# A fused attention and MLP kernel: q and k of the first eight blocks loaded in groups of four tokens, and another order of the opening

## The chip, the cores and the metric

The kernel runs on one core of a Trainium2 chip. The metric is the device time of one execution in microseconds; the median of 3 runs before the change is 1161.43 us (1158.59 to 1162.66). The engines are named as in the profile: PE (TensorE, with PEld for its weight loads), DVE (VectorE), ACT (ScalarE), POOL (GpSimd) and SP (SyncE, which here only issues DMAs).

## The reference, cut to what matters

Attention in chunks over q, k, v of shape 4 x 8 heads x 768 tokens x 64, then two MLPs of 512 x 2048 x 512 on the 3072 tokens. The weights are given in double precision.

```python
chunk, left_ctx, right_ctx = 32, 16, 8          # n_mem = 8
for c in range(nc):
    l_start = max(0, c_start - left_ctx)
    r_end = min(S, c_end + right_ctx)
    k_full = np.concatenate([mem_k, k[:, :, l_start:r_end]], axis=2)
    v_full = np.concatenate([mem_v, v[:, :, l_start:r_end]], axis=2)
    scores = scale * np.matmul(q_c, k_full.transpose(0, 1, 3, 2))
    scores = scores - np.max(scores, axis=-1, keepdims=True)
    a = np.exp(scores)
    a = a / (np.sum(a, axis=-1, keepdims=True) + 1e-09)
    out[:, :, c_start:c_end] = np.matmul(a, v_full)
...
h = x @ w_in;  x = np.maximum(0.01 * h, h) @ w_out           # first MLP
h = x @ w_in2; g = P(h) / (Q(h) + 1e-06); return g @ w_out2  # second MLP
```

Each chunk of 32 queries sees 64 keys: 8 memory rows and a span of 56 tokens (16 to its left, its own 32, 8 to its right). Spans of neighbouring chunks overlap by 24 tokens.

## The kernel before, in words

**MLP.** Tokens are cut into six tiles of 512. For every tile and each of 16 slices f of the hidden width, `emit_h` (L633) makes a bank hps of 128 x 512 by 12 matmuls (4 parts of the input width times three products of high and low halves: xh, xl for the activations, wih, wil for the weights), `leaky` (L645) turns it into gh and gl, and `emit_y` (L689) adds 12 matmuls into four banks acc. That is an item c; layer 0 has 96 of them, layer 1 another 96 (`rational` L656, `emit_o` L726). The items run in one loop (L792). Every item has two slots, 2c and 2c + 1: `wide(slot)` (L619) inserts attention work into slot 2c, which stands behind an `emit_h` and ahead of an `emit_y`, and into slot 2c + 1, behind that `emit_y`.

**Weights.** A half (w_in or w_out of one slice) is loaded by `load_w` (ld, L120) into one of three buffers wr, then `scale_w` (sc, ACT L139), `join_w` (jn, two DVE passes L153 and L156), `split_w` (ca, ACT L167, the high part) and the low part (lo, DVE L170). In the first token tile `weights0` (L180) does one such round twice per item, and a load waits until the join has freed its buffer. The high and low parts stand in 16 homes of their own for each of four kinds (`wpool`, L81).

**Attention.** A block j has 128 tokens of all 8 heads, four chunks; blocks 0 to 3 are the first token tile and are made in the opening, blocks 4 to 7 during the first token tile's items, the others later by another path (`wide_*`) which the change leaves alone. The steps of a block are: loads of q, k, v (q.ld, k.ld, v.ld); a, where PE transposes q and k (L319, L326) and ACT copies them to qT and kwT (L332, L335); s, the 64 small matmuls of scores (L347) and DVE's maximum and, for blocks 0 to 3, subtraction (L361, L363); e, the exponentials on ACT (L370, or eight short ones with their sums, L375, for blocks 4 to 7); n, DVE's normalisation (L384 to L389); p, four transposes of the weights by PE into a bank pst (L396) and ACT's copy pm (L400); x, 64 small matmuls with v (L414), ACT's copy to xh (L427) and DVE's xl (L431). q is loaded token by token, 256 bytes a piece, as 128 rows; k twice as 88 rows (a half block with its context), with memory rows above and below; v as eight loads of 56 rows, and memory rows by POOL's DMAs. Three places (`room`, L239) hold k and v of the blocks in turn; kwT and pwT are one buffer each.

**Order.** All engines run in the order in which the program issues. In the opening that is the list `OPENING` (L21): each word is one step of one block or of the weights. SP issues the loads in the list's order too. From block 4 on, `plan` (L578) puts block j's a into slot u = 1 + 6(j - 4), s and the next block's loads of q and k into u + 1, e into u + 2, n into u + 3, and p and x into the next block's u and u + 1, for block 7 into u + 4 and u + 5. Of PSUM's eight banks, four (acc) serve the MLP's sums and, in the opening, scores and x; the other four (ps) serve hps, the transposes, and blocks 4 to 7.

Of the kernel before, what the change touches and what calls it, by code (L numbers as in the profile page):

```python
# [30 lines left out]
def kernel(  # L31
# [49 lines left out]
    wpool = ctx.enter_context(tc.tile_pool(name="wpool", bufs=FC))  # L81
# [16 lines left out]
    small = const.tile([P, 14], F32, name="small")  # L98
    coef, ncf, babs = small[:, 0:6], small[:, 6:10], small[:, 10:12]
# [138 lines left out]
    spare = [xpool.tile([P, 2, 2 * H * D], F32R, tag=t, name=t).bitcast(F32) for t in ("xh", "xl")]  # L238
    room = [(kw, vflat), (spare[0][:, 0], spare[0][:, 1]), (spare[1][:, 0], spare[1][:, 1])]  # L239
    mem_in = {}  # L240
    mq, mqT, mm = {}, {}, {}

    def home(j):
        return j if j < len(room) else 0

    def mem_rows(kind, j, bi):
        if mem_in.get((kind, home(j))) == bi:
            return False
        mem_in[kind, home(j)] = bi
        return True  # L250

    def mid_load_q(j):
        bi, blk = divmod(j, WPS)
        if j < FIRST:
            t = wpool.tile([P, H * D], F32, tag=("wih", "wil", "woh", "wol")[j], name="q0")
        else:
            t = raw.tile([P, H * D], F32, tag="qr", name="qr", bufs=1)
        nc.sync.dma_start(out=t.rearrange("p (h d) -> p h d", h=H),
                          in_=q[bi, :, blk * P:(blk + 1) * P, :].rearrange("h p d -> p h d"))
        mq[j] = t  # L260

    def mid_mem_k(j):
        bi = j // WPS
        t = room[home(j)][0].rearrange("p (n h d) -> p n h d", n=2, h=H)
        if mem_rows("k", j, bi):
            for n in range(2):
                for row in (0, NM + CTX):
                    nc.gpsimd.dma_start(out=t[row:row + NM, n], in_=mem_k[bi].rearrange("h p d -> p h d"))

    def mid_load_k(j):  # L270
        bi, blk = divmod(j, WPS)
        mid_mem_k(j)
        t = room[home(j)][0].rearrange("p (n h d) -> p n h d", n=2, h=H)
        for n in range(2):
            at = blk * P + n * 2 * CHUNK - LCTX
            lo, hi = max(at, 0), min(at + CTX, S)
            nc.sync.dma_start(out=t[NM + lo - at:NM + hi - at, n],  # L277
                              in_=k[bi, :, lo:hi, :].rearrange("h p d -> p h d"))

    def mid_mem_v(j):  # L280
        bi = j // WPS
        t = room[home(j)][1].rearrange("p (n k h d) -> p k n h d", n=2, k=2, h=H // 2)
        W = WIN - NM
        if mem_rows("v", j, bi):
            for hh in range(2):
                for odd in range(2):
                    row = hh * WIN + odd * W
                    for n in range(2):
                        nc.gpsimd.dma_start(out=t[row:row + NM, odd, n],
                                            in_=mem_v[bi, 4 * hh:4 * hh + 4].rearrange("h p d -> p h d"))  # L290

    def mid_load_v(j):
        bi, blk = divmod(j, WPS)
        mid_mem_v(j)
        t = room[home(j)][1].rearrange("p (n k h d) -> p k n h d", n=2, k=2, h=H // 2)
        W = WIN - NM
        for hh in range(2):
            hs = slice(4 * hh, 4 * hh + 4)
            for odd in range(2):
                row = hh * WIN + (0 if odd else NM)  # L300
                at = blk * P + odd * CHUNK - LCTX
                for n in range(2):
                    a0 = at + n * 2 * CHUNK
                    lo, hi = max(a0, 0), min(a0 + W, S)
                    nc.sync.dma_start(out=t[row + lo - a0:row + hi - a0, odd, n],
                                      in_=v[bi, hs, lo:hi, :].rearrange("h p d -> p h d"))
# [7 lines left out]

    def mid_a_pe(j):
        t = mq.pop(j)
        ps = psw.tile([P, 512], F32, tag="ps", name="psq")
        for p in range(NP):
            nc.tensor.transpose(ps[:, p * P:(p + 1) * P], t[:, p * P:(p + 1) * P], ident)  # L319
        held["a", j] = [ps]  # L320
        t = room[home(j)][0]
        for n in range(2):
            ps = psw.tile([P, 512], F32, tag="ps", name="psk")[:, :NP * KW]
            for p in range(NP):
                f = n * H * D + p * P
                nc.tensor.transpose(ps[:, p * KW:(p + 1) * KW], t[:KW, f:f + P], ident[:KW, :KW])  # L326
            held["a", j].append(ps)

    def mid_a_act(j):
        psq, *psk = held.pop(("a", j))  # L330
        o = tmp.tile([P, NP, P], F32, tag="A", name="qT")
        nc.scalar.mul(out=o.rearrange("p c m -> p (c m)"), in_=psq, mul=scale)  # L332
        mqT[j] = o
        for n in range(2):
            nc.scalar.copy(out=kwT[:, n * NP * KW:(n + 1) * NP * KW], in_=psk[n])  # L335

    def mid_s_pe(j):
        qt = mqT.pop(j)
        kt = kwT[:, :2 * NP * KW].rearrange("p (n c m) -> p n c m", n=2, c=NP)
        ps = [mid_bank(j, "pss")[:, :NP * WIN].rearrange("p (n m) -> p n m", n=NP) for e in range(2)]  # L340
        for p in range(NP):
            at = 2 * (p % 2) + p // 2
            for e in range(2):
                r = slice(e * 64, e * 64 + 64)
                for c in range(NCH):
                    k0 = c % 2 * KOFF
                    nc.tensor.matmul(ps[e][c * CHUNK:(c + 1) * CHUNK, at, :], qt[r, p, c * CHUNK:(c + 1) * CHUNK],  # L347
                                     kt[r, c // 2, p, k0:k0 + WIN], start=True, stop=True)
        held["s", j] = ps

    def mid_s_dve(j):
# [47 lines left out]
    def mid_p_act(j):  # L399
        nc.scalar.copy(out=pwT, in_=held.pop(("p", j)))  # L400
# [470 lines left out]
```

## Time and profile before

| | us |
|---|---|
| median of 3 runs | 1161.43 |
| the profiled execution | 1160.44 |
| its span, first to last instruction | 1158.7 |
| PE busy in the span | 1132.8 |
| DVE, ACT, POOL busy | 728.2, 624.9, 249.2 |

The profile's times count from the first instruction of the span. A row of a timeline gives start, duration, engine, line, operation, output and inputs, shapes, the number of instructions merged into it, and in brackets how long the engine stood idle before it and what ended that. A PE row's duration has a tail in it: the distance between two starts is the pace.

### The profile page before, as it was taken

To read this page: it belongs to the slowest core of one execution; us is meant where nothing else is said; L and a number is where in the kernel's file an instruction comes from. 1 tells how busy PE (TensorE), PEld (TensorE's weight loads), DVE (VectorE), ACT (ScalarE), POOL (GpSimd) and SP (SyncE) were. 2 spreads that over 40 slices of the span, in tenths; PEclk is the share of its full clock that TensorE was granted. 3 is DMA by queue.
4 is the path that set the end of the run, shared out by engine and by line. 5 is a ranking of instruction groups with operands and counts; after the bars stand their busy time and mean duration, and the time that the engine had idled before them with its cause. 6 is when DMAs were issued, how large, how long until landed. Compare 5 with 4: busy or idle time off the path is not lost.

```text
span 1158.7 us, 20156 instructions
## 1 busy us (share of the span) xinstructions
PE 1132.8 (98%) x7808; PEld 929.8 (80%) x7808; DVE 728.2 (63%) x1297; ACT 624.9 (54%) x1135; POOL 249.2 (22%) x302
## 2 busy tenths in 40 slices
PE   6799899999999999999999999999999999999998
PEld 5678688888888888888888888888888888888887
DVE  4566644554454544443344888788788788788775
ACT  4567532332233223232345877777777777777765
POOL 7001031242122321120000222222222222222222
PEclk9999899999999999999999999999999999999999
DMA  9767777888777778753342200200200200200000
GB/s 170 194 188 198 210 200 192 217 224 244 199 198 235 208 209 237 195 161 105 95 145 73 91 1 1 73 1 1 73 1 1 73 1 1 73 1 1 37 1 37
DMA packets 148844, 132.18 MB, mean 114 GB/s; under 512 B 63281, under 2 KB 119185, under 8 KB 148749
## 3 DMA queue, kind: packets, MB, share of 16 engines
q1 hardware_dynamic: 142349, 122.90, 37.4%
q0 software_dynamic: 6400, 7.99, 3.0%
q8 instruction: 62, 1.02, 0.4%
q14 instruction: 33, 0.27, 0.1%
HBM read 93.06 MB, written 37.75 MB: 113 GB/s over the span
## 4 chain that ended last, share of the span: by engine, by line
PE 92%; DVE 2%; ACT 2%; DMA 2%; issue 1%; SPq 1%; ACTq 0%
PE hps L641 44%; PE acc L737 23%; PE acc L699 20%; PE psx L414 2%; PE pss L535 1%; DVE ww L156 1%; DMA vb<-in_v_dram 1%; ACT ww L139 1%; DMA xl<-in_k_dram 1%; ACT t L375 1%; DMA wr<-in_moe_w_out_dram 0%; DVE gl L654 0%; DVE wil L170 0%; PE psk L326 0%; SPq L277 0%
## 5 line engine op out<-in xcount | busy, mean ns | idle before, releaser
L677 POOL TENSOR_TENSOR gl<-R,gh 128x512 fp32r<-128x512 f32 x96 | 125.3, 1305 | 503.2 <-ACT gh L676 461.0
L651 ACT ACTIVATE gh<-hps 128x512 fp32r<-128x512 f32 x96 | 57.5, 599 | 301.4 <-PE hps L641 301.4
L654 DVE TENSOR_TENSOR gl<-s,gh 128x512 fp32r<-128x512 f32 x96 | 66.3, 690 | 211.6 <-ACT s L652 207.3
L641 PE MATMUL hps<-xh,wih 128*128 128x512 f32 x384 | 155.1, 404 | 1.9 <-ACT pm L400 1.4
L641 PE MATMUL hps<-xl,wih 128*128 128x512 f32 x384 | 151.6, 395 | 0.0
L641 PE MATMUL hps<-xh,wil 128*128 128x512 f32 x384 | 151.4, 394 | 0.0
L699 PE MATMUL acc<-gh,woh 128*128 128x512 f32 x384 | 150.9, 393 | 0.0
L699 PE MATMUL acc<-gh,wol 128*128 128x512 f32 x384 | 149.5, 389 | 0.0
L699 PE MATMUL acc<-gl,woh 128*128 128x512 f32 x384 | 149.5, 389 | 0.0
L641 PE MATMUL hps<-yh,wih 128*128 128x512 f32 x384 | 149.4, 389 | 0.0
L641 PE MATMUL hps<-yl,wih 128*128 128x512 f32 x384 | 149.4, 389 | 0.0
L641 PE MATMUL hps<-yh,wil 128*128 128x512 f32 x384 | 149.4, 389 | 0.0
L737 PE MATMUL acc<-woh,gh 128*128 128x512 f32 x384 | 149.4, 389 | 0.0
L737 PE MATMUL acc<-wol,gh 128*128 128x512 f32 x384 | 149.4, 389 | 0.0
L737 PE MATMUL acc<-woh,gl 128*128 128x512 f32 x384 | 149.4, 389 | 0.0
L500 POOL DMA_DIRECT2D vb<-in_v_dram x128 | 83.5, 653 | 253.7 <-PE psx L414 197.3
L664 ACT ACTIVATE A<-hps 128x512 f32<-128x512 f32 x96 | 57.1, 595 | 114.0 <-PE hps L641 114.0
L680 DVE SCALAR_TENSOR_TENSOR A<-A,small,pb 128x512 f32<-128x512 f32 x96 | 71.9, 749 | 56.4 <-ACT pb L665 56.3
L641 PEld LDWEIGHTS hps<-xh,wih 128*128 128x128 f32 x384 | 73.1, 190 | 19.6 <-ACT pm L400 2.0
L641 PEld LDWEIGHTS hps<-xh,wil 128*128 128x128 f32 x384 | 73.1, 190 | 15.6
L671 DVE SCALAR_TENSOR_TENSOR A<-A,pb 128x512 f32<-128x512 f32 x96 | 66.4, 692 | 30.3 <-ACT pb L684 30.3
L641 PEld LDWEIGHTS hps<-xl,wih 128*128 128x128 f32 x384 | 73.2, 191 | 14.8 <-DVE xl L431 0.4
(106 smaller groups left out, 1973.4 us busy)
## 6 DMA issues: line engine op xcount, KB each, us to landing
wr<-in_moe_w_in_dram SPq DMA_DIRECT2D x32, 512.0 KB
wr<-in_moe_w_out_dram SPq DMA_DIRECT2D x32, 512.0 KB
park_dram<-pb SPq DMA_DIRECT2D x16, 512.0 KB
pb<-park_dram SPq DMA_DIRECT2D x64, 128.0 KB
w_dram<-ww SPq DMA_DIRECT2D x32, 256.0 KB
wb<-w_dram SPq DMA_DIRECT2D x32, 256.0 KB
kb<-in_k_dram SPq DMA_DIRECT2D x59, 112.0 KB
vb<-in_v_dram POOLq DMA_DIRECT2D x118, 56.0 KB, 3.6
```

What stands on the lines that cost most here:

```text
L139: nc.scalar.activation(out=wsum[key], in_=wraw[key][:, :, 1].bitcast(F32), func=AF.Prelu, scale=2.0 ** -112, alpha=-2.0 ** 32)
L414: nc.tensor.matmul(ps[hh][e * 64:e * 64 + 64, i, c * CHUNK:(c + 1) * CHUNK], vt[r, c, 2 * i + e, :], weight(r, c, i, e), start=True, stop= ...
L500: nc.gpsimd.dma_start(out=vw[r + at:r + at + n, c], in_=v[bi, hs, lo:lo + n, :].rearrange("h p d -> p h d"))
L641: nc.tensor.matmul(ps[:, :n], w_[:, ws], x_[:, kk, :], start=(kk == 0 and m == 0), stop=(kk == KC - 1 and m == 2))
L651: nc.scalar.activation(out=gh, in_=ps, func=AF.Prelu, alpha=0.01)
L654: return [lambda: nc.vector.tensor_tensor(out=gl, in0=s, in1=gh.bitcast(F32), op=ALU.subtract)]
L664: nc.scalar.activation(out=A, in_=ps, func=AF.Square)
L671: nc.vector.scalar_tensor_tensor(out=A0, in0=A0, scalar=ONE, in1=U0, op0=ALU.add, op1=ALU.mult)
L677: nc.gpsimd.tensor_tensor(out=gl, in0=R0, in1=gh.bitcast(F32), op=ALU.subtract)
L680: nc.vector.scalar_tensor_tensor(out=A, in0=A, scalar=babs[:, 1:2], in1=U, op0=ALU.mult, op1=ALU.add)
L699: nc.tensor.matmul(acc[i][d][:, :n], w_[:, ws], g_, start=(f == 0 and m == 0), stop=(f == FC - 1 and m == 2))
L737: nc.tensor.matmul(acc[i][s], g_[:, ss], w_, start=(f == 0 and m == 0), stop=(f == FC - 1 and m == 2))
```

## The change

It touches the first eight blocks.

- Loads of q and k (`groups`): one DMA for the even heads and one for the odd ones. A row holds four consecutive tokens of one head, 1 KB; 128 rows are 4 heads x 32 groups. k is loaded once per block, from 8 tokens after the block's start to 8 after its end, not twice with overlap. The 8 rows of mem_k and, at the start of a sequence, the first 8 tokens of k come by a small load of their own (`mid_load_x`), on ACT's queue for block 0.
- a (`turn`): 8 matmuls with the identity as the moving operand for q and 8 for k, each 64 columns of the array wide, in place of 4 and 8 transposes. ACT's copies put the tokens back into order and write k as four full spans of 64 columns per head, one copy for the first span and one with overlapping reads for the other three; POOL copies the memory columns and the 24 columns that come from the block before.
- v's memory rows are loaded once, on ACT's queue, and spread by POOL's copies. v itself is loaded by eight DMAs as before.
- Blocks 0 to 3 have homes of their own for q, k, v, the turned k and the turned weights, in four large scratch tiles; the weights' homes become two tiles of eight slices for each kind, and the scratch is the second one's memory.
- Block 3 takes e in the eight short exponentials (`DIRECT`), without DVE's subtraction and sum.
- `OPENING` has another order, with 12 and 5 matmuls on a tile of zeros (`idle`) at the start and before block 2's p.
- `plan`: five slots per block, not six; block 7's p and x stand in u + 5 and u + 6.

```diff
+DIRECT = (3,)
 OPENING = """
-k0.ld q0.ld k1.ld q1.ld a0.pe v0.ld a0.act s0.pe ld a1.pe s0.dve q2.ld a1.act k2.ld e0.act s1.pe sc n0.dve
-v1.ld s1.dve p0.pe a2.pe p0.act q3.ld jn e1.act k3.ld x0.pe a2.act n1.dve x0.act ld s2.pe ca x0.dve p1.pe
-s2.dve v2.ld p1.act a3.pe lo e2.act n2.dve x1.pe a3.act v3.ld sc s3.pe x1.act jn ld p2.pe s3.dve p2.act ca ld
-x1.dve e3.act n3.dve x2.pe ld sc x2.act jn p3.pe sc x2.dve ld p3.act jn ca x3.pe sc lo ld q4.ld ca jn x3.act
-k4.ld x3.dve ca sc lo lo lo ld jn ld v4.ld
+m0.ld y0.ld q0.ld k0.ld q1.ld k1.ld v0.ld w12 a0.pe q2.ld a1.pe a0.act ld a1.act s0.pe k2.ld q3.ld s0.dve s1.pe
+k3.ld ld s1.dve e0.act a2.pe v1.ld n0.dve e1.act a3.pe a2.act n1.dve sc v2.ld s2.pe a3.act y1.ld y2.ld y3.ld
+s2.dve p1.pe p0.pe p1.act s3.pe ld jn e2.act x1.pe sc s3.dve p0.act v3.ld n2.dve e3.act jn w5 p2.pe ld x0.pe
+p2.act n3.dve x1.act x0.act x1.dve p3.pe ld x0.dve p3.act x2.pe ca sc x3.pe lo x2.act jn x3.act x2.dve ca
+x3.dve ca ld lo lo q4.ld k4.ld v4.ld sc jn ld ca lo sc jn ld ca lo sc jn ld
 """
-    wpool = ctx.enter_context(tc.tile_pool(name="wpool", bufs=FC))
+    wpool = ctx.enter_context(tc.tile_pool(name="wpool", bufs=2))
...
+    def w_home(n, f):
+        key = (n, f // FH)
+        if key not in wall:
+            wall[key] = wpool.tile([P, FH * DM], F32R, tag=n, name=n).rearrange("p (f m) -> p f m", f=FH)
+        return wall[key][:, f % FH, :]
...
+    def groups(issue, dst, x):
+        for e in range(2):
+            issue.dma_start(out=dst[:, e], in_=x.rearrange("(n e) (g t) d -> e n g (t d)", e=2, t=TK)[e])
...
+    def mid_load_x(j):
+        bi = j // WPS
+        t = raw.tile([P, H * D], F32, tag="qr", name="kx", bufs=1)[:XG].rearrange("p (e x) -> p e x", e=2)
+        issue = nc.sync if j else nc.scalar
+        groups(issue, t[:XG // 2], mem_k[bi])
+        groups(issue, t[XG // 2:], k[bi, :, 0:RCTX, :])
+        mkx[j] = t
     def mid_load_q(j):
         bi, blk = divmod(j, WPS)
...
+        groups(nc.sync, raw_home(j, 0), q[bi, :, blk * P:(blk + 1) * P, :])
...
+    def spread_v(dst, src):
+        for hh in range(2):
+            r = slice(hh * WIN, hh * WIN + NM)
+            nc.gpsimd.tensor_copy(out=dst[r], in_=src[r, 0:1].to_broadcast([NM, dst.shape[1], H // 2, D]))
...
+    def turn(t, n, j, name):
+        ps = psw.tile([P, 512], F32, tag="ps", name=name)
+        for i in range(TK):
+            for e in range(2):
+                nc.tensor.matmul(ps[e * D:(e + 1) * D, i * n:(i + 1) * n], t[:, e, i * D:(i + 1) * D], ident[:n, :n],
+                                 start=True, stop=True)
+        return ps[:, :TK * n]
     def mid_a_pe(j):
...
+        if j % WPS == 0:
+            held["m", j] = turn(mkx.pop(j), XG, j, "psm")
+        held["a", j] = [turn(raw_home(j, n), P, j, ("psq", "psk")[n]) for n in range(2)]
     def mid_a_act(j):
...
+        else:
+            nc.gpsimd.tensor_copy(out=kt[:, :, 0, NM:NM + LEFT], in_=k_home(j - 1)[:, :, NCH - 1, WIN - LEFT:])
+        if j <= FIRST or j % WPS == 0:
+            nc.gpsimd.tensor_copy(out=kt[:, :, :, :NM], in_=kmT.to_broadcast([P, NP, NCH, NM]))
...
+        nc.scalar.mul(out=o.rearrange("p n (g i) -> p n g i", i=TK), in_=psq, mul=scale)
...
+        nc.scalar.copy(out=kt[:, :, 0, NM + LEFT:].rearrange("p n (g i) -> p n g i", i=TK), in_=psk[:, :, :right // TK])
...
+        wins = bass.AP(tensor=src.tensor, offset=src.offset, ap=[part, heads, [CHUNK // TK, NCH - 1]] + rest)
+        nc.scalar.copy(out=kt[:, :, 1:, NM:].rearrange("p n c (g i) -> p n c g i", i=TK), in_=wins)
...
-            u = 1 + 6 * (j - FIRST)
+            u = 1 + 5 * (j - FIRST)
...
-                put(u + 4, lambda j=j: mid_p(j))
-                put(u + 5, lambda j=j: mid_x(j))
+                put(u + 5, lambda j=j: mid_p(j))
+                put(u + 6, lambda j=j: mid_x(j))
...
+        def idle(n):
+            ps = psw.tile([P, 512], F32, tag="ps", name="idle")
+            for _ in range(n):
+                nc.tensor.matmul(ps[:, :P], still, still, start=True, stop=True)
```

## Rows read from the trace of the kernel before

**Rows 1.** The page, part 2: busy tenths of PE in 40 slices.
```profile
PE   6799899999999999999999999999999999999998
```

**Rows 2.** Stretches: us, then busy us and instructions of each engine, PEclk, DMA.
```profile
0.00:44.77 44.77, 28.27 (x577) 23.13 (x577) 22.87 (x57) 19.70 (x38) 20.57 (x42) 1.00 0.85 176
...
135.00:145.20 10.20, 6.17 (x20) 4.58 (x20) 7.03 (x16) 2.25 (x5) 0.00 (x0) 0.67 0.68 208
145.20:1158.70 1013.50, 1009.77 (x6397) 830.53 (x6396) 639.91 (x1108) 542.50 (x931) 222.07 (x248) 1.00 0.36 103
```

**Rows 3.** Waits of PE from 45 to 200 us: total, times, longest.
```profile
PE pst L396 <- DVE t L389: 4.3, 1, 4.3
PE hps L641 <- ACT pm L400: 1.4, 3, 0.8
```

**Rows 4.** Timeline of PE, opening and first items.
```profile
24.10 1.18 PE L347 MATMUL pss<-pb,qT 64*32 64x64 f32 x64
...
42.38 1.93 PE L414 MATMUL psx<-pm,vb 64*64 64x32 f32 x64 [4.41 <-ACT pm L400]
44.77 0.79 PE L641 MATMUL hps<-xh,wih 128*128 128x512 f32 x1 [0.46 <-ACT xh L427]
...
49.74 0.39 PE L641 MATMUL hps<-xh,wil 128*128 128x512 f32 x1
...
52.48 0.39 PE L641 MATMUL hps<-xh,wil 128*128 128x512 f32 x1
...
58.15 0.60 PE L319 MATMUL psq<-ident,qr 128*128 128x128 f32 x4
...
59.24 0.48 PE L641 MATMUL hps<-xh,wih 128*128 128x512 f32 x1
...
62.17 0.86 PE L347 MATMUL pss<-pb,qT 64*32 64x64 f32 x64
...
76.69 0.60 PE L396 MATMUL pst<-ident,t 128*128 128x128 f32 x4
```

**Rows 5.** The chain of waits before the first hps: start, us, what.
```profile
35.61 5.55 DMA wr<-in_moe_w_out_dram
...
41.74 0.59 ACT pm L400
```

**Rows 6.** Timeline of DVE, opening and block 4.
```profile
17.17 0.42 DVE L361 TENSOR_REDUCE mx<-pss 128x4 f32<-128x256 f32 x1
...
18.75 0.41 DVE L153 TENSOR_SCALAR ww<-ww 128x512 uint32<-128x512 uint32 x1
...
19.80 0.68 DVE L384 TENSOR_REDUCE sm<-t 128x8 f32<-128x512 f32 x1
...
20.96 0.69 DVE L389 TENSOR_TENSOR t<-t,sm 128x512 f32<-128x512 f32 x1
24.61 0.76 DVE L431 TENSOR_TENSOR xl<-psx,xh 128x256 fp32r<-128x256 f32 x2 [2.96 <-ACT xh L427]
...
75.74 0.69 DVE L389 TENSOR_TENSOR t<-t,sm 128x512 f32<-128x512 f32 x1
```

**Rows 7.** A stretch with loads of weights alone; last columns DMA share and GB/s.
```profile
38.00:40.00 2.00, 0.00 (x0) 0.00 (x0) 0.00 (x0) 0.18 (x1) 0.00 (x0) 1.00 1.03 381
```

**Rows 8.** DMA view from 9 to 12 us, pieces of 256 bytes.
```profile
DMA packets 1820, 0.45 MB, mean 150 GB/s; under 512 B 1786, under 2 KB 1817, under 8 KB 1820
```

**Rows 9.** The page, part 6: a DMA's size and median us to landing.
```profile
vb<-in_v_dram POOLq DMA_DIRECT2D x118, 56.0 KB, 3.6
```

**Rows 10.** Timeline of SP's queue: issues of v.
```profile
6.71 5.31 SPq L305 DMA_DIRECT2D vb<-in_v_dram  x8
...
25.65 4.68 SPq L305 DMA_DIRECT2D xl<-in_v_dram  x8
```

**Rows 11.** Groups of POOL's instructions by line: busy us, mean ns.
```profile
L677 POOL TENSOR_TENSOR gl<-R,gh 128x512 fp32r<-128x512 f32 x96 | 125.3, 1305 | 503.2 <-ACT gh L676 461.0 <-issue 38.1 <-PE acc L737 4.1
...
masks.py:199 POOL TENSOR_SCALAR_AFFINE_SELECT ident<-ident 128x128 f32<-128x128 f32 x1 | 0.3, 292 | 0.1
```

More of the change, by code (lines that the diff above doesn't have):

```diff
@@ L237 @@
     LAST = WIDE_FROM * FIRST
[L238 to L250, printed above, removed]
+    TK = 4
@@ L270, in mid_load_k @@
     def mid_load_k(j):
         bi, blk = divmod(j, WPS)
[L272 to L278, printed above, removed]
-    def mid_mem_v(j):
[L281 to L290, printed above, removed]
+        lo = blk * P + RCTX
@@ new lines, in mid_load_k @@
+        hi = min(lo + P, S)
+        t, x = raw_home(j, 1), k[bi, :, lo:hi, :]
+        if hi == lo + P:
+            groups(nc.sync, t, x)
+        else:
+            x = x.rearrange("(n e) (g t) d -> n g e (t d)", e=2, t=TK)
+            for n in range(NP):
+                nc.sync.dma_start(out=t[n * BG:n * BG + (hi - lo) // TK], in_=x[n])
+    def spread_v(dst, src):
+        for hh in range(2):
+            r = slice(hh * WIN, hh * WIN + NM)
+            nc.gpsimd.tensor_copy(out=dst[r], in_=src[r, 0:1].to_broadcast([NM, dst.shape[1], H // 2, D]))
@@ L292, in mid_load_v @@
+    def mid_mem_v(j):
+        dst = v_home(j)
+        if 0 < j < FIRST:
+            spread_v(dst, v_home(0))
+            return
+        for hh in range(2):
+            nc.scalar.dma_start(out=dst[hh * WIN:hh * WIN + NM, 0],
+                                in_=mem_v[j // WPS, 4 * hh:4 * hh + 4].rearrange("h p d -> p h d"))
+        spread_v(dst[:, 1:], dst)
     def mid_load_v(j):
         bi, blk = divmod(j, WPS)
-        mid_mem_v(j)
-        t = room[home(j)][1].rearrange("p (n k h d) -> p k n h d", n=2, k=2, h=H // 2)
@@ L296, in mid_load_v @@
[L296 to L306, printed above, removed]
+        if j == FIRST or j > FIRST and j % WPS == 0:
+            mid_mem_v(j)
@@ L308, in mid_bank @@
+        t = v_home(j)
+        for c in range(NCH):
+            lo, at, n = window(blk, c)
+            for hh in range(2):
+                r = hh * WIN + at
+                nc.sync.dma_start(out=t[r:r + n, c],
+                                  in_=v[bi, 4 * hh:4 * hh + 4, lo:lo + n, :].rearrange("h p d -> p h d"))
     def mid_bank(j, name):
@@ L313 @@
     held = {}
-    def mid_a_pe(j):
[L316 to L327, printed above, removed]
@@ L331, in mid_a_act @@
         o = tmp.tile([P, NP, P], F32, tag="A", name="qT")
-        nc.scalar.mul(out=o.rearrange("p c m -> p (c m)"), in_=psq, mul=scale)
+        nc.scalar.mul(out=o.rearrange("p n (g i) -> p n g i", i=TK), in_=psq, mul=scale)
         mqT[j] = o
-        for n in range(2):
-            nc.scalar.copy(out=kwT[:, n * NP * KW:(n + 1) * NP * KW], in_=psk[n])
+        nc.scalar.copy(out=kt[:, :, 0, NM + LEFT:].rearrange("p n (g i) -> p n g i", i=TK), in_=psk[:, :, :right // TK])
+        g = (CHUNK - LEFT) // TK
@@ L337, in mid_s_pe @@
+        src = psk[:, :, g:g + (WIN - NM) // TK]
+        part, heads, *rest = [list(x) for x in src.ap]
+        wins = bass.AP(tensor=src.tensor, offset=src.offset, ap=[part, heads, [CHUNK // TK, NCH - 1]] + rest)
+        nc.scalar.copy(out=kt[:, :, 1:, NM:].rearrange("p n c (g i) -> p n c g i", i=TK), in_=wins)
     def mid_s_pe(j):
-        qt = mqT.pop(j)
-        kt = kwT[:, :2 * NP * KW].rearrange("p (n c m) -> p n c m", n=2, c=NP)
+        qt, kt = mqT.pop(j), k_home(j)
         ps = [mid_bank(j, "pss")[:, :NP * WIN].rearrange("p (n m) -> p n m", n=NP) for e in range(2)]
@@ L399, in mid_p_act @@
     def mid_p_act(j):
-        nc.scalar.copy(out=pwT, in_=held.pop(("p", j)))
+        nc.scalar.copy(out=p_home(j), in_=held.pop(("p", j)))
     def mid_x_pe(j):
-        pt = pwT.rearrange("p (e i c m) -> p e i c m", e=2, i=2, c=NCH)
-        weighted(j, room[home(j)][1].rearrange("p (c h d) -> p c h d", c=NCH, h=H // 2),
+        pt = p_home(j).rearrange("p (e i c m) -> p e i c m", e=2, i=2, c=NCH)
+        weighted(j, v_home(j),
                  lambda r, c, i, e: pt[r, e, i, c, :], mid_bank)
```

78 lines of the change are left out of this document (50 added, 28 removed).

## Prediction

> **What bounds the kernel now.** I read the page's slices first. TensorE (PE) is at 6 to 7 tenths in the first slice, at 9 in nearly all others, with one dip to 8 [rows 1]. The stretches say the same in time: 28.27 us busy of the first 44.77, 6.17 of the 10.2 around 140 us, and 1009.77 of the last 1013.5 [rows 2]. So the end moves only by what the opening takes before the first matmul of the MLP (44.77 us), by stalls after it, and by work added to PE. The waits of PE after the opening are two: 4.3 us once, a transpose of weights (pst) behind VectorE's normalisation, and 1.4 us in three waits of hps for a bank that ACT empties [rows 3]. PE's timeline in the opening shows the rest: after tile 3's pst it waits 4.41 us before the last psx, and hps starts at 44.77 [rows 4]. The chain puts that wait down to a weight transfer: in ACT's order a scale stands ahead of the copy pm, and waits for w_out until 41.2 [rows 5].
>
> The clock counts too. The granted clock reads 1.00 in the opening [rows 2], but the durations say otherwise: from 44.77 to 49.74 eleven steps of hps take 4.97 us (0.45 each), from 49.74 twelve take 2.74 (0.228) [rows 4]. That is the 1.2 GHz level, then 2.4; it costs 2.5 us. The dip at 140 us is the same: 4.3 us idle, then a mean granted clock of 0.67 [rows 2].
>
> **The change, opening.** All 16 loads of q and k get a quarter as many, four times longer pieces, each block gets its own home, and the order is new. Three sums decide when hps starts.
>
> VectorE. It cannot begin before s0. Twelve dummy matmuls of 128 columns in f32 (four passes, so like 512 columns: 0.43 us cold) run from about 1.1 to 6.2 us, while the loads come; SP needs 8 issues of some 0.42 for tiles 0 and 1, ACT 4 for the memory rows after its table load. Then a0 and a1. The turn by plain matmuls is not in the trace. It streams 16 x 128 columns per tile in two halves of the array, 1024 columns each; pss streams 64 x 64 in eight parts, 512 each, in 0.86 us [rows 4]. So 1.7 us warm. The lower end is the transposes that it replaces, 1.09 us from 58.15 to 59.24 [rows 4], less a fifth: 0.9; the upper end is 3.4, no overlap of the halves. I take 1.7, pss being nearest. With 0.4 for the memory rows, a0, a1 and s0 end at 6.5 + 0.4 + 3.4 + 0.8 = 11.1 us. From there VectorE has, up to the last xl: s three times 1.58 (17.17 to 18.75) and once 0.84, as tile 3 leaves the additions to ACT; n three times 1.85 (19.80 to 20.96 + 0.69) and once 1.1; jn three times 1.05 (18.75 to 19.80); one lo, a pass like the last of n, 0.7; four xl of 0.67 (a pair, 24.61) [rows 6]. That is 5.6 + 6.65 + 3.15 + 0.7 + 2.7 = 18.8, so 29.9 us without a gap. I allow 2.6 us for gaps: hps at 32.5.
>
> DMA. q and k of four tiles are 2.1 MB, three weight halves 1.6 MB; such larger pieces moved at 381 GB/s [rows 7], so 9.7 us. v stays in 256-byte pieces: 1.84 MB at the 150 GB/s of a stretch full of them [rows 8] is 12.3 us. A v load of 56 KB lands 3.6 us after its issue [rows 9], and SP starts at 0.75, so v3 is there at 26.4; x3 wants it at about 28. Hidden, with 1.6 us to spare; without that cover hps moves with v3, us for us.
>
> SP's queue. 16 loads of q and k at 0.42, 32 of v, three weights at 0.4. The v issues took 0.66 each in one row and 0.59 in another [rows 10], with the transfers behind them full; at 0.5 that is 0.75 + 6.7 + 16 + 1.2 = 24.7 us, and v3 lands at 28.3, just in time; at 0.66 it is 29.8 and 33.4, and with x3, xh and the wait between them hps starts at 36. I take 0.5, since fewer pieces stand in front of v, and keep 36 as the upper end of the opening.
>
> ACT is not the limit: it was busy 19.70 of the 44.77 us [rows 2], its two copies of k become a short and a long one, and only tile 3's exponentials, now eight, are more. POOL's new copies lie between 0.29 us (128x128, one input) and 1.3 (128x512, two inputs) [rows 11]; I take 0.4 for those of k, which s waits for, and 1 us for each spread of v's memory rows, which x needs 10 us later. At 2.6 us a spread, tile 0's two would hold up the copy of k behind them in POOL's queue and s0 by 3 us; that is inside the same bound.
>
> So the opening ends 44.8 - 32.5 = 12.3 us earlier (8.8 to 14.8). The five cold microseconds of the first hps I leave as they are; if the five dummies before p2 keep the clock up, 2.5 more go.
>
> **The change, MLP stage.** Tiles 4 to 7 now start every 5 slots, not 6, and the last p stands two slots behind its n instead of one. What goes: the 4.3 us stall and its cold stretch (twelve hps at 0.43 for 0.23, 2.4 us), as tile 7's p gets one slot more; and most of the 1.4 us, since a tile takes three banks where it took four, and hps finds one. Together 7.8. What comes: the turn, 4 x (1.7 - 1.1) and 0.4 for tile 6's memory rows, 2.8 us (0 to 10). And two new waits. In tile 4 the normalisation ends at 76.43 (75.74 + 0.69) and PE wants it at 76.69 [rows 4, 6]: 0.26 to spare at three slots. A slot is 12 matmuls of 0.228, 2.74 us; at two slots p comes 2.5 us too early. Tile 6 starts in an odd slot as well, so the same: 5.0 us for both (0 to 8.6). Behind the waiting p on PE stand a of the next tile and hps; ACT and VectorE lose nothing, as p waits for them. Tiles 5 and 7 start in even slots: there s stands behind a y and not right behind an h, so VectorE has that h's passes behind it and takes s at once; I give them no wait. Net: 2.8 + 5.0 - 7.8 = 0, between -6 and +6. The later parts are the same instructions; homes of weights in half tiles change only addresses, so I cost them at nothing: ACT's split is held by the readers of its own part, as psx's banks and kwT's halves are now (PE starts pss before the second half is copied). If the whole tile held it, ACT would wait for every h, which is the fourth case below.
>
> **Sum.** 1160.44 us is the profiled execution, 1158.7 its span; the median of the runs is 1161.43, 1 us above. 1161.4 - 12.3 + 0 = 1149.
>
> **Rivals.** First, four engines instead of sixteen. A group load's source runs over four heads, then 32 groups; the loads of before run over the tokens first. If such a DMA is moved by four of the 16 engines, 381/16 = 23.8 GB/s each [rows 7] give 95 GB/s: the 2.1 MB take 22 us on four engines, which also carry their share of v (12.3) and weights (4.2), so v3 lands at 41 and hps starts at 44 to 47, no gain. In the MLP stage each tile's 0.52 MB holds these four for 5.5 us, where before it was 0.62 MB at 150 [rows 8], 4.1 us, on all; weight halves queue behind it, the join chain has no slack, so up to 1.4 us and more per tile, 4 us in all: 1161.4 + 1 + 3 to 4 = 1165, slower. It decides when loads of q run at under 100 GB/s. For it: all the other loads have one outer dimension on both sides. Against it: no row shows a load of this form.
>
> The Trainium skill (DMA: Bandwidth & Descriptors, section on why a DMA increments its semaphore by 16) states that a DMA is spread over the largest number of engines, up to 16, that divides the slowest dimension of both sides; by that rule it would be four here, and this rival's time. No row of this trace shows or refutes it.
>
> Second, the clock stays at the lower level through the opening. For it: in the opening PE is busy 28 of 45 us and yet pss takes 1.18 us where it later takes 0.86 [rows 2, 4]. Against it: the dummies and the turn are plain matmuls. Cold, a tile is 3.4 + 1.1 + 0.9 + 1.9 us, four are 29, with 2.1 for the second dummies and 0.8: 6.5 + 32 = 38.5, hps at 39, 1155.5.
>
> Third, the start does not move, because the weights do not come earlier: ACT scales w_in's third half before x2's copy. If SP gets to it only at 36 us, as before (35.61 is a weight's issue [rows 5]), hps stays near 43 to 44: 1160.
>
> Fourth, false waits on the half-tile homes: ACT's splits behind each h, 0.5 us and more in 13 items of the first round: 8 us, 1157 with the opening's gain.
>
> **How the numbers follow.** Forecast 0.55, four engines 0.22, clock 0.14, start unmoved 0.06, homes 0.03. The forecast's own range is 1144 to 1155 (opening 30 to 36, MLP -6 to +6, not both at their ends). Over all cases 1144 to 1162 leaves out the upper half of the four engines and little below. A difference of 0.3%, 3.5 us, is what a measurement of this kernel can tell. Faster by more: nearly all of the forecast, three quarters of the clock's case and some of the rest, 0.69. Within it: 0.17, most of it from the four engines and the unmoved start. Slower: 0.14.
>
> **What would show it.** hps starting near 32 us, VectorE without gaps from 11 us, loads of q and k landing within 3 us of issue, two waits of pst for t of some 2.5 us (tiles 4 and 6) and no stretch at 0.67 clock. Wrong: q landing 5 us and more after issue, hps at 40 or later, a pst wait over 4 us, or a turn of 3 us in the MLP stage.

## The result, and the profile after

The changed kernel takes 1177.27 us (median of 4 runs, 1176.17 to 1178.02), the kernel before 1161.64 us beside it: a ratio of 1.0138 [1.0117, 1.0159], 1.4% slower, where 1149 was forecast. The profiled executions, which all rows come from, took 1176.17 us with a span of 1174.4 us, against 1160.44 and 1158.7 before: 15.7 us more.

The page's slices of the changed kernel, answering to [rows 1], nearly hide it: PE's first three are 6, 8, 8 tenths where they were 6, 7, 9. The granted clock (PEclk) reads 7, 7, 9 and 8 tenths in the first four, where the page of before reads 9. That is no difference to build on: by the durations of [rows 4] PE ran at the lower level in the opening of before too, up to 49.74 us. First the page of the changed kernel, then the clock on that of before:

```profile
PE   6889999999999999999999999999999999999998
...
PEclk7798999999999999999999999999999999999999
```

```profile
PEclk9999899999999999999999999999999999999999
```

The stretches (start:end, length, busy us and instructions of PE, PEld, DVE, ACT, POOL, then PEclk, DMA share, GB/s), cut at the first hps:

```profile
0.00:49.55 49.55, 34.48 (x706) 29.86 (x706) 18.37 (x51) 18.36 (x50) 10.26 (x21) 0.76 0.50 136
49.55:140.00 90.45, 81.45 (x844) 65.29 (x844) 51.18 (x101) 51.79 (x138) 6.15 (x9) 0.90 0.56 166
140.00:1174.40 1034.40, 1030.00 (x6499) 846.69 (x6484) 657.15 (x1145) 556.34 (x969) 222.47 (x248) 1.00 0.37 106
```

The MLP starts at 49.55 us instead of 44.77 [rows 2]: 4.8 us of the loss. From there to the end it is 1124.9 us against 1113.9: the other 10.9, in the 90 us in which blocks 4 to 7 run beside it. The DMA share of the opening is 0.50 where it was 0.85 [rows 2]: the transfers are late, and yet the DMA engines stand half idle.

The timeline of VectorE (start, duration, ..., idle time before it and its releaser) has the consequence in two lines. It begins at 18.70 us, not at 11.1, and stands 10.10 us between tiles 1 and 2:

```profile
18.70 0.11 DVE L395 MEMSET pss<- 32x64 f32 x1 [16.84 <-PE pss L384]
...
35.96 0.42 DVE L398 TENSOR_REDUCE mx<-pss 128x4 f32<-128x256 f32 x1 [10.10 <-PE pss L384]
```

PE's timeline, answering to [rows 4]: most of the memory rows and then the first q are turned only from 11.73 us; hps runs at the 1.2 GHz level until 53.48 (nine steps in 3.93 us); a turn of q and k takes 0.92 and 0.97 us at the upper level; and in the MLP stage PE waits again:

```profile
11.73 1.03 PE L344 MATMUL psm<-ident,kx 16*64 16x16 f32 x14 [3.14 <-DMA kx<-in_k_dram]
12.69 1.98 PE L344 MATMUL psq<-ident,scratch_wih 128*64 128x128 f32 x16
...
49.55 0.80 PE L680 MATMUL hps<-xh,wih 128*128 128x512 f32 x1 [0.43 <-ACT xh L464]
...
53.48 0.40 PE L680 MATMUL hps<-xh,wih 128*128 128x512 f32 x1
...
62.44 1.09 PE L344 MATMUL psq<-ident,kb 128*64 128x128 f32 x16
63.36 1.04 PE L344 MATMUL psk<-ident,kb 128*64 128x128 f32 x16
64.33 0.50 PE L680 MATMUL hps<-xh,wih 128*128 128x512 f32 x1
...
83.20 0.63 PE L433 MATMUL pst<-ident,t 128*128 128x128 f32 x4 [3.96 <-ACT gh L690]
...
107.74 1.80 PE L344 MATMUL psk<-ident,kb 128*64 128x128 f32 x14 [1.56 <-DMA kb<-in_k_dram]
```

The waits of PE from 60 to 200 us (total, times, longest) answer to [rows 3]: a wait for k's load, which did not exist before, and 5.9 us for the transposes of weights.

```profile
PE pst L433 <- ACT gh L690: 5.9, 2, 4.0
PE psk L344 <- DMA kb<-in_k_dram: 2.4, 3, 1.6
```

Of the 5.9 us for the transposes, 5.2 remain in e1 below, where the loads are fast: they come with the spacing. What the loads themselves do is in the chain (start, us, what), which before had one such piece of 5.55 us in the opening [rows 5]. In the MLP stage a load of a weight half takes 4.5 and 8.5 us, and one of k 7.4 us, from issue to landing:

```profile
58.13 4.52 DMA wr<-in_moe_w_in_dram
...
100.24 8.54 DMA wr<-in_moe_w_out_dram
...
125.96 7.38 DMA kb<-in_k_dram
```

The half of 100.24 stands in SP's queue behind eight group loads (memory rows, q and k of tile 6, issued from 95.09 to 100.13); the k that lands late at 133.3 is itself one. ACT waits 6.1 us for that half, and all that ACT does for PE is behind it:

```profile
108.86 0.67 ACT L151 ACTIVATE ww<-wr 128x512 f32<-128x512 f32 x1 [6.12 <-DMA wr<-in_moe_w_out_dram]
```

### The profile page after: what moved, and what is told of

It reads as the page before. It is cut to its first block, busy times and chain, and to the rows that moved or that the text cites. A ratio compares the mean times of both kernels' runs of the same rounds, so it can differ in the third digit from the quotient of the medians.

```text
span 1174.4 us, 20581 instructions
## 1 busy us (share of the span) xinstructions
PE 1145.9 (98%) x8034; PEld 941.8 (80%) x8034; DVE 726.7 (62%) x1295; ACT 626.5 (53%) x1154; POOL 238.9 (20%) x278
## 4 chain that ended last, share of the span: by engine, by line
PE 90%; DMA 5%; ACT 2%; DVE 1%; SPq 1%; issue 1%; ACTq 0%
PE hps L680 43%; PE acc L776 22%; PE acc L738 21%; PE psx L451 2%; DMA scratch_wih<-in_k_dram 1%; DMA wr<-in_moe_w_out_dram 1%; PE pss L572 1%; SPq L277 1%; DMA vb<-in_v_dram 1%; DMA kb<-in_k_dram 1%; ACT ww L151 1%; DVE ww L168 1%; DMA scratch_wil<-in_v_dram 1%; PE psk L344 0%; ACT t L412 0%
## 5 line engine op out<-in xcount | busy, mean ns | idle before, releaser
L680 PEld LDWEIGHTS hps<-xh,wil 128*128 128x128 f32 x384 | 73.1, 190 | 15.7
L738 PEld LDWEIGHTS acc<-gh,woh 128*128 128x128 f32 x384 | 72.2, 188 | 15.9 <-issue 0.7
```

The lines of the kernel that those rows point to most:

```text
L680: nc.tensor.matmul(ps[:, :n], w_[:, ws], x_[:, kk, :], start=(kk == 0 and m == 0), stop=(kk == KC - 1 and m == 2))
L738: nc.tensor.matmul(acc[i][d][:, :n], w_[:, ws], g_, start=(f == 0 and m == 0), stop=(f == FC - 1 and m == 2))
```

## The experiments

The theory after the trace was the first rival of the prediction, at a higher price: loads whose source runs over four heads first are slow, in the opening and in the MLP stage. The rivals to it were the spacing of five slots and the order of the opening. In the table, each ratio is to the kernel before as it ran beside that version (medians of 1161.0 to 1162.0), hps is the start of the first hps in the profile and "rest" the profile's span less that.

| kernel | median us | ratio to before | hps | rest |
|---|---|---|---|---|
| before | 1161.64 | 1 | 44.77 | 1113.9 |
| changed | 1177.27 | 1.0138 [1.0117, 1.0159] | 49.55 | 1124.9 |
| e1_groups_outer | 1156.18 | 0.9962 [0.9950, 0.9975] | 36.97 | 1116.1 |
| e2_six_slots | 1176.27 | 1.0125 [1.0110, 1.0140] | 50.24 | 1124.6 |
| e3_before_five | 1159.17 | 0.9981 [0.9972, 0.9990] | 47.03 | 1111.4 |
| e4_outer_six | 1154.13 | 0.9929 [0.9906, 0.9953] | 34.48 | 1112.7 |
| e5_two_heads | 1220.93 | 1.0513 [1.0484, 1.0541] | 71.16 | 1148.3 |
| e6_turned_opening | 1167.43 | 1.0049 [1.0033, 1.0065] | 36.09 | 1130.6 |
| e7_turned_mlp | 1169.82 | 1.0068 [1.0047, 1.0090] | 51.05 | 1116.8 |
| e8_no_dummies | 1152.63 | 0.9924 [0.9906, 0.9942] | 37.09 | 1114.3 |
| e9_v1_pool | 1157.65 | 0.9971 [0.9959, 0.9982] | 42.13 | 1112.4 |
| e10_v1_pool_early | 1153.10 | 0.9934 [0.9911, 0.9957] | 37.87 | 1112.3 |
| e11_early_start | 1152.47 | 0.9926 [0.9903, 0.9949] | 37.32 | 1112.5 |
| e12_v_last | 1152.79 | 0.9937 [0.9916, 0.9958] | 35.34 | 1114.0 |

A start of hps from one profile is good to some 2 us only: the openings of e1, e4 and e6 are the same instructions and start hps at 36.97, 34.48 and 36.09; those of before and e3 at 44.77 and 47.03; those of the changed kernel, e2 and e7 at 49.55, 50.24 and 51.05.

**e1: the order of the loads' source turned.** The groups come first, then the heads. The bytes, their pieces (1 KB) and the number of loads of the opening stay; ACT's copies and the windows of k read the turned result in the other order. (Block 5's short k goes through the same function, two loads for four.)

```diff
-            issue.dma_start(out=dst[:, e], in_=x.rearrange("(n e) (g t) d -> e n g (t d)", e=2, t=TK)[e])
+            issue.dma_start(out=dst[:, e], in_=x.rearrange("(n e) (g t) d -> e g n (t d)", e=2, t=TK)[e])
...
-            for n in range(NP):
-                nc.sync.dma_start(out=t[n * BG:n * BG + (hi - lo) // TK], in_=x[n])
+            groups(nc.sync, t[:(hi - lo) // TK * NP], x)
...
-        psq, psk = (ps.rearrange("p (i n g) -> p n g i", i=TK, n=NP) for ps in held.pop(("a", j)))
+        psq, psk = (ps.rearrange("p (i g n) -> p n g i", i=TK, n=NP) for ps in held.pop(("a", j)))
```

> The changed kernel with one thing turned round: the loads of q and k name the 32 groups of tokens first and the four heads second (row = 4 x group + head), and ACT's copies read the turned banks in that order; same bytes, same 1 KB pieces, same number of DMAs but three fewer for block 5's k. Theory (a load whose source runs over four heads first is moved by four of the 16 DMA engines): all 16 move it, q and k of tile 0 land within 4 us of issue, hps starts at 31 to 37 us instead of 49.6, and the time is 1150 us (1145 to 1158). Rival 1 (the loads are slow for another reason: 1 KB pieces, the issue on SP, the scattered rows): hps stays at 47 or later and the time above 1170. Rival 2 (the opening is bound by the low clock and the order): hps at 42 to 48, time 1165 to 1172.

Measured: 1156.18 us, 21.1 less than the changed kernel; hps at 36.97. That is 0.4% faster than before, and the time expected was 1150 (1145 to 1158). Both rivals fall. The view of the DMAs from 8 to 30 us, in 40 slices (tenths of 16 engines' time, then GB/s), shows what changed. In the changed kernel, where group loads stand alone, it lies flat at 2 tenths and 86 to 95 GB/s:

```profile
DMA  2222235323645723621268995222222222257999
GB/s 94 95 93 89 91 110 154 107 91 108 183 124 117 157 48 83 145 27 19 63 184 235 311 315 125 86 91 93 91 91 91 93 91 91 93 136 162 328 290 240
```

With the order turned no such flat stretch remains. Group loads, v and weight halves mix here; the slices of 382 and 387 GB/s are, by the order of issue, mostly a weight half that SP issued at 12.20 us:

```profile
DMA  4765644417769999886789999835555465205699
GB/s 95 161 138 127 144 100 101 134 21 197 116 143 382 387 363 335 255 203 201 136 257 367 311 248 220 171 82 115 124 129 119 111 143 117 48 14 85 140 385 367
```

Stretches with little but group loads in flight tell more (columns as in the stretches above; the last two are the DMA share and GB/s). First the changed kernel; then e1 with its first eight loads of q and k, and, by the order of issue, with k2 and q3 behind that weight half:

```profile
23.00:27.00 4.00, 2.45 (x18) 1.68 (x16) 2.69 (x7) 0.60 (x1) 0.00 (x0) 0.50 0.27 91
```

```profile
2.50:8.00 5.50, 5.35 (x45) 5.00 (x46) 0.00 (x0) 0.27 (x2) 0.64 (x1) 1.00 0.69 196
15.70:17.20 1.50, 0.27 (x2) 0.29 (x2) 1.40 (x4) 1.08 (x2) 0.00 (x0) 0.83 1.00 329
```

A share of 0.27 is 4.3 of sixteen engines; turned, it is 11 and then all 16. 91 is a quarter of 381 [rows 7] to within 5%: four of sixteen engines. The 196 GB/s lie near the pace of SP's issues, an estimate from its rows: 128 KB every 0.62 us are 211 GB/s.

**e2: the changed kernel with six slots.**

```diff
-            u = 1 + 5 * (j - FIRST)
+            u = 1 + 6 * (j - FIRST)
```

> The changed kernel with blocks 4 to 7 every six slots again (block 7's p and x keep the later place). Theory (four engines): the opening stays as it is, hps at 49.6; in the MLP stage the waits of PE become fewer, as each block's loads have 3 us more, but weights still queue behind them: 1170 to 1174. Rival (the five-slot spacing alone makes the 11 us by which the MLP stage got longer): all of it comes back, 1166.

Measured: 1176.27, 1 us less, and above either expectation. The longest pst wait went from 4.0 to 1.5 us, but 2.5 us of psk for its load stayed, and pss now waits 2.1 us for ACT's copy. PE's waits from 60 to 200 us did not become fewer: 10.6 us in all for 9.3. While the loads are slow, the spacing gives back nothing that can be told.

**e3: the kernel before with five slots.** The spacing alone, with the last p and x one slot later.

```diff
-            u = 1 + 6 * (j - FIRST)
+            u = 1 + 5 * (j - FIRST)
...
-                put(u + 4, lambda j=j: mid_p(j))
-                put(u + 5, lambda j=j: mid_x(j))
+                put(u + 5, lambda j=j: mid_p(j))
+                put(u + 6, lambda j=j: mid_x(j))
```

> The kernel before with the five-slot spacing alone (and block 7's p and x one slot later). My sum: block 7's stall and its cold stretch go (6.7 us), two waits of pst of 2.5 us come (blocks 4 and 6): 1160 (1157 to 1163). Rival (the spacing is what makes the MLP stage longer): 1168 to 1172.

Measured: 1159.17, 0.2% less than before (1162.04 in this set), as the theory had it: the one wait of 4.3 us [rows 3] gives way to two that sum to 4.4, and the rest is 2.5 us shorter.

```profile
PE pst L396 <- ACT gh L651: 4.4, 2, 2.5
```

**e4: turned loads and six slots,** the edits of e1 and e2 together.

> Both: groups first in the loads, and six slots a block. Theory: the opening of the first run (hps at 31 to 37), no wait of pst over 1 us in the MLP stage: 1146 (1142 to 1154), 2 to 5 us under the five-slot one. Rival 1 (loads slow for another reason): above 1165. If the spacing costs nothing with good loads, the two agree within 2 us.

Measured: 1154.13 (1149.11 to 1154.94), 8 us above the 1146 expected, just past the end of its range. It beats both kernels. Against e1 the rest is 3.4 us shorter, as the two waits of pst are down to 1.6 and 0.9: with fast loads the spacing counts after all. By the medians it is worth 2.05 us; the profile is of e4's fastest execution (1149.11, the next took 1153.37), so 3.4 is on the high side. The rows are the waits of PE from 60 to 200 us, first of e1, then of e4:

```profile
PE pst L431 <- ACT gh L688: 5.2, 2, 3.1
PE pss L570 <- ACT s L689: 1.8, 1, 1.8
```

```profile
PE psx L449 <- ACT pm L435: 1.6, 1, 1.6
PE pst L431 <- ACT gh L688: 1.6, 1, 1.6
PE pst L431 <- DVE t L424: 0.9, 1, 0.9
```

**e5: two heads instead of four.** Turning the order might also have helped by where the pieces lie in memory. So the other way round: each group load of the changed kernel cut into two loads of two heads.

```diff
-            issue.dma_start(out=dst[:, e], in_=x.rearrange("(n e) (g t) d -> e n g (t d)", e=2, t=TK)[e])
+            y = x.rearrange("(n e) (g t) d -> e n g (t d)", e=2, t=TK)[e]
+            r = y.shape[0] * y.shape[1] // 2
+            for m in range(2):
+                issue.dma_start(out=dst[m * r:(m + 1) * r, e], in_=y[2 * m:2 * m + 2])
```

> The changed kernel with each group load of q and k cut into two loads of two heads each (same bytes, same pieces, twice the issues). In the changed kernel such loads move at a flat 91 to 94 GB/s with a DMA share of 0.2 to 0.3 of the 16 engines. Theory (the slowest dimension sets the number of engines): two engines for each load now. If the second load goes to the same two engines, some 46 GB/s with a share of 0.12, hps at 65 us or later and over 1190 us; if it goes to two others, 91 GB/s as before, and only the issues come on top: hps at 50 to 54, 1177 to 1185. Rival (the four heads lie far apart in memory and that makes the pieces slow, on all engines): two heads are no slower, 91 GB/s or more at a share over 0.25, hps at 47 to 51 and 1172 to 1180.

Measured: 1220.93, 43.7 us more than the changed kernel, hps at 71.16. The same view of the DMAs, from 8 to 30 us, lies flat at half of the former rate:

```profile
DMA  1111111111111111111111111222344434331510
GB/s 47 45 48 45 45 47 47 45 45 59 46 45 47 47 43 46 47 47 55 48 45 47 45 46 46 82 69 77 84 123 118 109 102 114 74 87 34 129 10 13
```

Four heads give 91 GB/s, two give 46, both 23 per head; and two such loads in the queue do not add up to 91, so the second one does not run beside the first on other engines. A stretch of e5 has the share, 0.13 or 2.1 of sixteen engines:

```profile
4.00:13.00 9.00, 2.62 (x13) 2.35 (x13) 0.00 (x0) 0.00 (x0) 0.00 (x0) 0.87 0.13 46
```

The place in memory is out as a cause. This is the rule that the Trainium skill states (DMA: Bandwidth & Descriptors, section "Why a DMA increments its semaphore by 16 and not by 1"): the number of engines is the largest up to 16 that divides the slowest dimension of both sides. The shares of 4.3 and 2.1 engines for first dimensions of four and two agree. It also says that for a load issued from SP or ACT these are the lowest-numbered ones; the flat 46 GB/s of e5 agrees.

**e6 and e7: turned in one stage only.** In e6 the order is turned for tiles 0 to 3, in e7 for tiles 4 to 7; a condition on j picks the order in the load and in the reading of its result.

```diff
+        order = "e g n (t d)" if turned(j) else "e n g (t d)"
...
-            issue.dma_start(out=dst[:, e], in_=x.rearrange("(n e) (g t) d -> e n g (t d)", e=2, t=TK)[e])
+            issue.dma_start(out=dst[:, e], in_=x.rearrange("(n e) (g t) d -> " + order, e=2, t=TK)[e])
```

> The changed kernel with the order of the loads' source turned (groups first, then heads) for tiles 0 to 3 alone. Theory (slow loads cost in both places): hps starts at 37 us as with all loads turned, and from there on all is as in the changed kernel (1124.9 us to the end): span 1162, time 1165 (1161 to 1168). Rival (all of the loss in the MLP stage comes down from the late opening, since weights and tiles start late): 1156 to 1158, as with all loads turned.

> The changed kernel with the order of the loads' source turned (groups first, then heads) for tiles 4 to 7 alone. Theory (slow loads cost in both places): hps starts at 49.5 us as in the changed kernel, the rest takes 1116 us as with all loads turned: span 1166, time 1168.5 (1165 to 1172). Rival (the loss of the MLP stage comes down from the late opening): 1174 to 1178, no gain over the changed kernel.

Measured: 1167.43 and 1169.82, both within the theory's ranges. The opening alone gives back 9.8 us, the MLP stage alone 7.4; both together 21.1. The parts fall short by 4 us because of e6: its hps starts 13.5 us earlier, but the rest is 5.7 us longer than in the changed kernel, 1130.6. What is slow there seems to collide with more: psk waits 3.9 us for its loads where it was 2.4, and pss 1.4 for a load of the later path; the rest of the 5.7 was not traced. Waits of PE from 60 to 200 us in e6:

```profile
PE pst L439 <- ACT gh L696: 6.0, 2, 4.1
PE psk L350 <- DMA kb<-in_k_dram: 3.9, 3, 1.7
PE pss L578 <- DMA pb<-park_dram: 1.4, 1, 1.4
```

In e7 psk waits for no load, and the rest is 1116.8, as in e1.

**e8: no dummy matmuls** (e4 without `w12` and `w5` in `OPENING`).

> The version with turned loads and six slots, without the 17 dummy matmuls of the opening. Theory (the dummies hold the clock at the upper level, from 6.7 us on in that version): the turns of tiles 0 and 1 run cold (1.7 us for 16 matmuls instead of 0.92, four of them before VectorE starts), hps at 36 to 38 instead of 34.5, time 1156 to 1158. Rival (the turns raise the clock by themselves and the loads set the start): hps at 34 to 35, 1153 to 1155.

Measured: 1152.63, the rival's number with the theory's start: hps at 37.09. The first turns do run at the lower level (1.98 us where e4 has 1.09), and VectorE starts at 15.27 instead of 12.41; the median is not above e4's. In this opening a VectorE that starts 2.9 us later costs nothing that shows.

```profile
8.10 1.98 PE L342 MATMUL psq<-ident,scratch_wih 128*64 128x128 f32 x16
```

**e9 and e10: v of tile 1 issued by POOL,** on e8. In e10 tile 0's q and k are moreover turned before its memory rows, and s0 stands before the turns of tile 1.

```diff
-                nc.sync.dma_start(out=t[r:r + n, c],
+                (nc.gpsimd if j == 1 else nc.sync).dma_start(out=t[r:r + n, c],
```

> The version with turned loads, six slots and no dummies, with the eight loads of v of tile 1 issued by POOL instead of SP. There SP issues v1 and v2 from 17.1 to 26.6 us and v3 and the weights behind them, so that they wait for SP's queue. Theory (SP's issues set the end of the opening): v3 and the third half of w_in are issued some 4 us earlier and hps starts 2 to 3 us earlier than 37.1: 1150 (1147 to 1152). Rival (VectorE's chain from s0 sets it): hps at 36 to 38, 1152 to 1154.

> As the version with v1 on POOL; moreover tile 0's q and k are turned before the memory rows, which land last, and s0 stands before the turns of tile 1. Theory (VectorE, busy almost without gaps from its start at 12.4 us, sets the end of the opening once v and the weights come earlier): VectorE starts at 10.5 to 11 us and hps 1 to 2 us before the version with v1 on POOL alone: 1148.5 (1146 to 1151). Rival (SP's queue or the transfers still set it): the same time as that version.

Both missed. e9 takes 1157.65, 5 us more than e8. POOL's timeline shows why: after three of the eight loads it stands 3.10 us, after three more 3.24, and the copies of k that s2 needs come behind them at 25.16, where e8 has them at 15.46. s2 follows at 25.72 us, 4.6 us after e8's (21.09). The rows are of e9, and last e8's copy. What POOL waited for in those gaps the trace does not name.

```profile
13.20 2.11 POOL L325 DMA_DIRECT2D scratch_wil<-in_v_dram  x3
18.40 1.93 POOL L325 DMA_DIRECT2D scratch_wil<-in_v_dram  x3 [3.10 <-issue]
23.58 0.65 POOL L325 DMA_DIRECT2D scratch_wil<-in_v_dram  x1 [3.24 <-issue]
24.51 0.66 POOL L325 DMA_DIRECT2D scratch_wil<-in_v_dram  x1 [0.29 <-issue]
25.16 0.28 POOL L359 COPY scratch_woh<-scratch_woh 128x96 f32<-128x96 f32 x1
```

```profile
15.46 0.27 POOL L359 COPY scratch_woh<-scratch_woh 128x96 f32<-128x96 f32 x1 [2.19 <-ACT scratch_woh L371]
```

In e10 VectorE starts at 10.97 and these copies come at 19.85; it takes 1153.10, no better than e8. A queue that is free of issues is not free of cost if its engine's own work comes behind them.

**e11 and e12: VectorE earlier, then v last,** on e4. e11 turns tile 0's q and k before the memory rows and moves dummies; e12 also issues q and k of all four tiles before any v. The diff is of the list in e12, against the changed kernel's:

```diff
-m0.ld y0.ld q0.ld k0.ld q1.ld k1.ld v0.ld w12 a0.pe q2.ld a1.pe a0.act ld a1.act s0.pe k2.ld q3.ld s0.dve s1.pe
-k3.ld ld s1.dve e0.act a2.pe v1.ld n0.dve e1.act a3.pe a2.act n1.dve sc v2.ld s2.pe a3.act y1.ld y2.ld y3.ld
+m0.ld q0.ld k0.ld q1.ld k1.ld w8 a0.pe q2.ld a1.pe a0.act k2.ld q3.ld k3.ld a1.act y0.ld s0.pe ld s0.dve s1.pe
+v0.ld ld s1.dve e0.act a2.pe v1.ld n0.dve e1.act a3.pe a2.act n1.dve sc v2.ld s2.pe a3.act y1.ld y2.ld y3.ld
...
-p2.act n3.dve x1.act x0.act x1.dve p3.pe ld x0.dve p3.act x2.pe ca sc x3.pe lo x2.act jn x3.act x2.dve ca
+p2.act n3.dve x1.act x0.act x1.dve p3.pe ld x0.dve p3.act w5 x2.pe ca sc x3.pe lo x2.act jn x3.act x2.dve ca
```

> The version with turned loads and six slots, all v issued by SP. Tile 0's q and k are turned before the memory rows, whose transfers land last; the spread of v's memory rows of tile 0 goes behind tile 1's copies in POOL's queue; eight dummy matmuls instead of twelve at the start, and five more before the last two psx. Theory (VectorE's chain from s0 sets hps, and the copies of POOL and the memory rows set s0): VectorE starts at 10.5 to 11.2 us instead of 12.4, hps at 32.5 to 33.5 instead of 34.5, and the dummies before psx keep the clock at the upper level there (34.0 to 37.4 was at the lower one, 1.7 us): 1151 (1148 to 1153). Rival (v and the weights, which SP issues at the same times as before, set hps): hps at 34 to 35.5, 1152 to 1155.

> As the version with the early start of VectorE, with the loads of q and k of all four tiles issued before any load of v. There VectorE began at 10.5 us but stood 5.3 us before tile 2, since the eight v loads of tile 0 stood ahead of q2 and k2 and their transfers ran at 111 to 160 GB/s. Theory (the order of the transfers sets hps now): VectorE goes on from tile 1 to tile 2 with a gap under 2 us, v3 is issued by 28 us, hps at 32 to 34: 1149 (1146 to 1151). Rival (the sum of v's transfers and issues sets it, in whatever order they stand): v3 lands no earlier, hps at 36 to 38, 1151 to 1154.

Measured: 1152.47 and 1152.79, the rivals' times. VectorE starts at 10.5 us in both, 1.9 before e4, yet hps at 37.32 and 35.34: in e11 VectorE stands 5.33 us before tile 2, in e12 3.37 before the first normalisation. The dummies before psx work (hps is at the upper level within 0.8 us in both), and still the time stays. Five versions with turned loads and six slots (e4, e8, e10 to e12) thus lie at 1152.5 to 1154.1, whichever of these is moved. In each of their chains the last 4 to 6 us before hps are the last pst, psx and one copy of ACT, and ahead of them stand VectorE's joins of weights and its normalisations; which wait sets them was not settled.

## Why the prediction was wrong

**The step that failed is the DMA term of the opening:** "such larger pieces moved at 381 GB/s [rows 7], so 9.7 us". The row it took, [rows 7], was of weight loads, whose first dimension is 128. Here it was 91 GB/s, and 2.1 MB of q and k take 23 us at it. With that, a0 began at 12.69 us, VectorE at 18.70 instead of 11.1, and the start of hps was 49.55, 17 us past the 32.5 forecast. SP's issues were held up with the loads: v3's last issue ended at 43.94 us, for 24.7 in the sum and 31.29 in e1. The rows are of the changed kernel and of e1:

```profile
39.69 4.25 SPq L327 DMA_DIRECT2D scratch_wil<-in_v_dram  x8
```

```profile
27.18 4.11 SPq L325 DMA_DIRECT2D scratch_wil<-in_v_dram  x8
```

With the loads turned and the opening otherwise the same, hps starts at 34.5 to 37.0 (e1, e4, e6), so what was left of that sum was 2 to 4.5 us too hopeful. Two of its terms were off: SP took some 0.62 us to issue a group load (e1, two in 1.25) for 0.42, and VectorE, which began at 11.99 us in e1, stood 5.42 us before tile 2 where all gaps together were allowed 2.6. Which of them held hps is open: neither v3 issued by 29.63 us (e10) nor VectorE begun at 10.5 (e11, e12) brought the time down.

**The second step that failed is "Net: 2.8 + 5.0 - 7.8 = 0" for the MLP stage;** the same loads put it at +10.9. Taken apart by e1, 8.7 us of it are the slow loads (1124.9 against 1116.1), and 2.2 are the terms that the sum had. Two of those held: the turn took 1.89 us per tile (62.44 to 64.33) for 1.7; the two new waits of pst sum to 5.2 us for 5.0 (e1). The profile puts them down to gh and not to t, but at the first of them, in e1, t ends at 69.57 us and gh at 69.62, so t was late as the sum had it. Six slots bring them down to 2.5 us (e4); the rest of the versions with six slots and turned loads, 1112.3 to 1114.3, is about that of before.

**The first rival was right, and its price was not.** It had the mechanism, its rate (95 GB/s for 91) and its sign, at a chance of 0.22 and 1165 us. hps at 44 to 47 was 49.55, and "3 to 4" in the MLP stage was 8.7. Its price counted how long a tile's loads hold the four engines and let the weight halves queue behind them for the difference, 1.4 us a tile. It left out how far that reaches: a weight half that lands 8.54 us after its issue holds ACT for 6.1 us; PE stands in that time, 1.56 us for k's own load and 0.51 for ACT's copy, and then runs at the lower level:

```profile
107.70:115.00 7.30, 6.75 (x26) 5.19 (x26) 4.04 (x7) 3.66 (x9) 0.53 (x1) 0.53 0.41 125
```

From 49.55 to 140 PE is busy 81.45 us at a mean granted clock of 0.90; in e1, in a stretch as long, 84.54 us at 0.98:

```profile
36.97:127.00 90.03, 84.54 (x887) 68.32 (x888) 58.43 (x117) 59.39 (x163) 6.31 (x9) 0.98 0.62 184
```

Busy time times clock is 73.3 against 82.8 us: by this estimate 9.5 us of work at full speed, of which about a third is standing (9.0 us against 5.5) and two thirds are clock.

**The chance** rested on "Against it: no row shows a load of this form". That no row shows a form is no evidence against a rule about that form. Whether the rule's condition is met could be read from the access pattern alone: four was its first dimension.

**The other rivals.** The clock stayed low in parts of the opening (0.76 in the mean, cold at hps), but as a result of the waits: with the loads turned it reads 0.91 (e1), and taking the dummies out cost nothing (e8). The spacing was priced rightly (e3). Of false waits on the half-tile homes the trace shows none: ACT's splits (L178) wait for VectorE's joins alone, 14.2 us from 49 to 200 us, and PE for no home. The unmoved start is not what happened.

## What to carry to other kernels

Read every new load by its access pattern, not by its bytes: with a first dimension of four it moved at 91 GB/s, a quarter of what weight loads reached, and exchanging two dimensions in the source (and reading the result in the other order) was worth 21 us here. A slow load costs more than its own lateness: price what stands behind it in the same queue, who waits for that, and the clock after PE has stood. And where a queue is relieved by moving issues to another engine, look at what that engine has to compute behind them.

## What was not expected of the hardware

The rate went with the first dimension: 46 GB/s for two and 91 for four, within a few per cent, and for 32 groups up to some 329, where other loads had left them a queue. POOL stopped for 3.1 and 3.2 us after every three loads of v (e9; 2.2 and 2.1 in e10), while SP issued such loads one after another at 0.45 to 0.6 us each (e8: 8 in 3.60 us, 16 in 9.49).
